# The second half of w_in by seven products instead of eight, with its scale measured during attention

## The chip, the cores and the metric

One core of one Trainium2 chip runs the whole kernel. The metric is the device time of the launch in microseconds, the median over the runs shown, lower being better. Five engines work from queues of their own and meet only at semaphores: TensorE (matrix products; PE in the profile, and PEld for the loading of its stationary operand), VectorE (DVE), ScalarE (ACT), GpSimd (POOL) and SyncE (SP, which issues most DMAs). Each takes its instructions in the order in which they were written; one that waits holds up all behind it on that engine.

## The reference, cut to what matters

The input x has 2048 tokens of 1024 features. Two blocks follow each other, each on a normalized input and added back to it:

```
h  = x + A(layernorm(x))     # causal attention in 4 segments of 512 tokens, 32 heads, with a running memory
h2 = h + B(layernorm(h))
B(x):  z  = gelu(x @ w_in)              # w_in: 1024 x 3584
       z1 = z[:, :1792]                 # first half
       z2 = layernorm(z[:, 1792:])      # second half, normalized per token
       g  = w_sp @ z2 + b_sp            # w_sp: 2048 x 2048, mixes tokens
       out = (z1 * g) @ w_out           # w_out: 1792 x 1024
```

The change concerns the second half of x @ w_in, the 2048 x 1024 by 1024 x 1792 product in front of z2.

## The kernel before, in words

A recorder (`_Recorder`) keeps the operations of each engine in the order of the Python calls and works out the waits from the tiles that are read and written; the profile therefore gives line 210 for nearly everything, and one has to go by tile names. The order written in Python is the order on each engine; nothing is reordered later.

**Attention** is a loop of 32 steps, n = 0 to 31: segment s = n // 8, a group of four heads c = n % 8. A step issues three rounds of logits into PSUM banks 0 to 3 (`logits`; the third round also puts the memory product `om` there, `mem`), and ACT takes each round out with an exp into tile `e`; POOL then masks `e` (`affine_select`). DVE takes `om` out in `mem_norm` (tiles `rdm`, `tm`), and the logits of the next step overwrite these banks. The products of the step before (`pv`, banks 4 and 5) are taken out by DVE in `norm` (tiles `rd`, `ta`, `otok`). Between these stand fillers: the projections of the next step (`qk`, taken out by ACT, in segment 0 by DVE), and in slots f3 and f4 the V projection (taken out by ACT) or, in steps c = 2 to 5, the output projection of the segment before (`wo`, taken out by DVE into `hch`, followed by a layernorm in tasks that `bg_pop` advances). Fillers use banks 6 and 7 in turn. `phi_max` prepares the next step's `pqk` on DVE at the end of the step.

**z2 stage.** w_in's second half is loaded in four chunks of 448 columns (`win`). `z2_group(k, tc)` multiplies 128 tokens with one chunk in eight matmuls of 448 columns; ACT takes the bank out with a gelu into `Z2`, and `z2_stats` sums it on DVE for the layernorm (`bn_stats`, tile `zst`). 4 chunks x 16 token tiles x 8 give 512 matmuls, 48 of them as fillers of steps 30 and 31. Between them stands `wo` of the last segment. Beside them run: the squares of w_sp's 16 row blocks on ACT (`sp_norm`, tile `sj`), the maxima of w_in's first half on DVE (`wz_norm`, 14 reductions into `sqz`), its scaled f16 copies (`wz_half`), the differences of the normalized input (`hn_sum`, tiles `ht` and `z1x`) and sums of the weights on POOL (`sz_sum`).

**z1 stage.** The first half is already computed by seven block products instead of eight (a scheme of Strassen's kind): `z1_step(g, k)` is product k of group g, four matmuls of 512 columns; 14 groups of 7. Product 1 is copied by ACT to `zt`, and DVE adds it to the banks (five additions a group). The rest of the layernorm is applied to Z2 here, alternately on DVE and ACT (`z2_apply`).

Then follow the token mix (`gate`) for the first 1024 tokens, 16 output units, `gate` for the other 1024, and the last output products; all of these are as before in the change, up to the addresses of buffers.

Of the kernel before, what the change touches and what calls it, by code (L numbers as in the profile page):

```python
# [12 lines left out]
T = 2048  # L13
D = 1024
# [244 lines left out]
def bass_sequential_preLN__memory_aug_infini_attn__mixer_gmlp__prompt_kernel(  # L259
# [31 lines left out]
    class Bump:  # L291
# [4 lines left out]
        def __call__(self, name, shape, dt):  # L296
# [50 lines left out]
    ZSTG = [tens("zstg%d" % i, [128, 448], F32, (134 + 2 * i) * K) for i in range(4)]  # L347
    XCH = [b2("xch%d" % i, [128, D], BF16) for i in range(4)]
# [4 lines left out]
    E = [[b2("e%d%d" % (k, i), [128, 4, w], BF16) for i, w in enumerate((512, 512, 256))] for k in range(2)]  # L353
    TA = b2("ta", [128, 4, 4, 32], F32)
    TM = [b2("tm%d" % i, [128, 4, 4, 32], F32) for i in range(2)]
    V = b2("v", [128, 4, H, 34], BF16)
    OTOK = [b2("otok%d" % i, [128, 4, D], BF16) for i in range(2)]


    WIN = [tens("win%d" % i, [128, 8, 512], BF16, o * K) for i, o in enumerate((46, 54, 190, 198))]  # L360
# [9 lines left out]
          for k, o in ROLES + (("t1", 118), ("t2", 190), ("t3", 22), ("t4", 38))}  # L370
    SS = tens("ss", [128, 4, 8, 128], F16, 30 * K)
    Z1X = tens("z1x", [128, 14, T], F16, 62 * K)
    HT = [{1: Z1X[:, 1:5, 1024:1536], 2: Z1X[:, 1:5, 1536:2048], 3: Z1X[:, 8:12, 1024:1536],
           4: Z1X[:, 8:12, 1536:2048]},
          {1: tens("ht1", [128, 4, L], F16, 190 * K), 2: tens("ht2", [128, 4, L], F16, 194 * K),
           3: tens("ht3", [128, 4, L], F16, 38 * K), 4: tens("ht4", [128, 4, L], F16, 198 * K)}]
    SZ = [tens("sz%d" % i, [128, 4, 128], F16, o * K) for i, o in enumerate((58, 59, 60, 61, 204))]
    ZT = [tens("zt%d" % i, [128, L], F32, o * K) for i, o in enumerate((4, 6, 8, 10, 202, 12))]
# [7 lines left out]
    SQ = b3("sq", [128, 16], F32)  # L386
    SQZ = b3("sqz", [128, 14], F32)
# [8 lines left out]
    TMP = {k: tens("tmp_" + k, [128, L], F32, (4 + 2 * i) * K)  # L396
           for i, k in enumerate(("s1", "s1b1", "s1b2", "u2", "u3"))}
    VB = tens("vb", [128, L], BF16, 61 * K)
    SJ = [tens("sj%d" % i, [128, T], BF16, (4 + 4 * i) * K) for i in range(2)]
    BROW = [tens("brow%d" % i, [128, L], BF16, (205 + i) * K) for i in range(2)]  # L400
    WO0 = [tens("w_out0%d" % i, [128, 7, 512], BF16, o * K) for i, o in enumerate((54, 198))]
    WO1 = [tens("w_out1%d" % i, [128, 7, 512], BF16, o * K) for i, o in enumerate((30, 4))]
# [3 lines left out]
    SY = [tens("sy%d" % i, [128, 4, 7, 128], F16, o * K) for i, o in enumerate((190, 126))]  # L406
    FIN = [tens("fin%d" % i, [128, 512], BF16, o * K) for i, o in enumerate((37, 11, 12, 13))]
# [13 lines left out]
    def next_bank():  # L421
        b = rot["banks"][rot["n"] % len(rot["banks"])]
        rot["n"] += 1
        return b
# [382 lines left out]
    CH = [(FH + 448 * k, 448) for k in range(4)]  # L807

    def win_load(k):
        lo, w = CH[k]  # L810
        sp.dma_start(WIN[k][:, :, 0:w], wcols(B_w_in, lo, lo + w))

    zs, zq, staged = [], [], []

    def z2_group(k, tc, stage=None):
        s, tcl = divmod(tc, 4)
        b = next_bank()
        wi = WIN[k]
        mm8(PS[:, b, 0:448], lambda i: HNT[s][:, i, tcl * 128:(tcl + 1) * 128], lambda i: wi[:, i, 0:448])
        if stage is None:  # L820
            z2_gelu(k, tc, PS[:, b, 0:448])
        else:
            act.activation(ZSTG[stage][:], PS[:, b, 0:448], ACTF.Copy)
            staged.append((k, tc, ZSTG[stage][:]))

    def z2_gelu(k, tc, src):
        act.activation(Z2[:, tc, k * 448:(k + 1) * 448], src, ACTF.Gelu_apprx_tanh)
        zs.append((k, tc))

    def z2_stats():  # L830
        k, tc = zs.pop(0)
        dve.bn_stats(ZST[:, tc, k, :], Z2[:, tc, k * 448:(k + 1) * 448])
        if k == 3:
# [13 lines left out]

    LAST = NSEG * NQ - 1
    for n in range(LAST + 1):
# [13 lines left out]
        elif c < 2:  # L863
            f3, f4 = [("v", s, 2 * c, 1)], [("v", s, 2 * c + 1, 1)]
        elif c < 6:
            f3, f4 = [("wo", s - 1, c - 2, 0)], [("wo", s - 1, c - 2, 1)]
        elif c == 6:
            f3, f4 = [("z2", 0, 4, 0)], [("z2", 0, 5, 1)]
        else:
            f1, f2 = [("z2", 0, 6, 2)], [("z2", 0, 7, 3)]  # L870
            f3, f4 = [("z2", 0, 0)], [("z2", 0, 1)]
# [14 lines left out]
        if n == 0:  # L886
# [3 lines left out]
            f3 = [("vmm", 0, 0, 1, 6, 2, 8), ("vout", 0, 0, 1, 6)]  # L890
        logits(n, 0)
# [12 lines left out]
        if n < LAST:  # L904
            phi_exp(n + 1)
        if n == 0:
# [9 lines left out]
        bg_pop()  # L916
        if n == 0:
# [3 lines left out]
        if n in (24, 26):  # L921
            win_load((n - 24) // 2)
    pv(LAST)
    xr_load(4 * (NSEG - 1))


    rot["banks"] = [0, 1, 2, 3, 6, 7, 4, 5]
    rot["n"] = 0
    win_load(2)

    pool.memset(ONES[:], 1.0)
    pool.memset(MHZ[:], -0.5)

    def sp_norm_load(r):
        sp.dma_start(SJ[r % 2][:], B_w_sp[r * 128:(r + 1) * 128, :])

    def sp_norm(r):
        act.activation(SJ[r % 2][:], SJ[r % 2][:], ACTF.Square, accum_out=SQ[:, r:r + 1])

    def scale_of(k, n, b):  # L940
        b = next_bank() if b is None else b
        pe.matmul(PS[:, b, 0:n], ONES[:], SQB[:, 0:n], start=True, stop=True)
        dve.tensor_reduce(out=TOT[:], in_=PS[:, b, 0:n], axis=mybir.AxisListType.X, op=ALU.add)
        dve.tensor_single_scalar(TOT[:], TOT[:], 1e-30, ALU.max)
        if k:
            dve.reciprocal(TOP[:], TOT[:])
        else:
            pool.tensor_tensor(TOP[:], TOT[:], MHZ[:], ALU.pow)

    def scale_end(k):  # L950
        dve.tensor_single_scalar(TOP[:].bitcast(I32), TOP[:].bitcast(I32), 0x7F800000, ALU.bitwise_and)
        dve.tensor_single_scalar(SC[k][:], TOP[:], 8192.0, ALU.mult)
        dve.reciprocal(INV[k][:], SC[k][:])

    def wz_load(q):
        w = 256 if q < 3 else 128
        for i in range(2):
            lo = 896 * i + 256 * q
            sp.dma_start(WZ[q][:, :, i, :], wcols(B_w_in, lo, lo + w))

    def wz_norm(q, r):
        v = WZ[q][:, 2 * r:2 * r + 2, :, :] if q < 3 else WZ[q][:, 4 * r:4 * r + 4, :, :]
        dve.tensor_reduce(out=SQZ[:, 4 * q + r:4 * q + r + 1], in_=v.rearrange("p c i w -> p (c i w)"), axis=mybir.AxisListType.X, op=ALU.max,
                          apply_absolute_value=True)

    def wz_half(q, h):
        dve.tensor_single_scalar(WZH[q][:, 4 * h:4 * h + 4], WZ[q][:, 4 * h:4 * h + 4], SC[1][:], ALU.mult)

    def hb(j, k, p):
        return HNT[2 * p + k][:, 4 * j:4 * j + 4, :]  # L970

    def hn_sum(p, t, h, eng=dve):
        a, b = {1: (hb(0, 1, p), hb(0, 0, p)), 2: (hb(1, 1, p), HT[p][1][:]),
                3: (hb(1, 1, p), hb(0, 1, p)), 4: (hb(1, 0, p), HT[p][2][:])}[t]
        s = slice(2 * h, 2 * h + 2)
        eng.tensor_tensor(HT[p][t][:, s, :], a[:, s, :], b[:, s, :], ALU.subtract)

    def wz_blk(i, j, fc):
        o = 128 * (fc % 2)
        return WZH[fc // 2][:, 4 * j:4 * j + 4, i, o:o + 128]  # L980

    def sz(g, k):
        return SZ[k - 1 + (k == 4 and g % 2)][:]

    def sz_sum(g, k):
        fc = g % 7
        a, b, op = {1: (wz_blk(1, 0, fc), wz_blk(1, 1, fc), ALU.add), 2: (sz(g, 1), wz_blk(0, 0, fc), ALU.subtract),
                    3: (wz_blk(0, 0, fc), wz_blk(1, 0, fc), ALU.subtract),
                    4: (wz_blk(0, 1, fc), sz(g, 2), ALU.subtract)}[k]
        pool.tensor_tensor(sz(g, k), a, b, op)  # L990

    aux = {}

    def at(q, f, *a):
        aux.setdefault(q, []).append((f, a))

    for r in range(16):
        q = (37 * r + 15) // 16
        at(q, sp_norm, r)
        if r < 14:  # L1000
            at(q, sp_norm_load, r + 2)
    at(37, pool.tensor_copy, SQB[:, 0:16], SQ[:])
    for k in range(12):
        at(k + 1, wz_norm, (1, 2, 0)[k // 4], k % 4)
    for k in range(8):
        at(3 + 2 * k, hn_sum, 0, (1, 2, 3, 4)[k // 2], k % 2)
    at(18, wz_norm, 3, 0)
    at(19, wz_norm, 3, 1)
    at(20, pool.tensor_copy, SQB[:, 0:14], SQZ[:])
    at(25, scale_of, 1, 14, None)  # L1010
    at(25, scale_end, 1)
    for k in range(8):
        at(26 + k, wz_half, k // 2, k % 2)
    for k in range(4):
        at(28 + 2 * k, hn_sum, 1, 1 + k // 2, k % 2)
    for k in (1, 2, 3, 4):
        at(28 + k, sz_sum, 0, k)

    todo = [(0, 2), (0, 3), (0, 8), (0, 9), 0, (0, 10), 1, (0, 11), 2, (1, 0), 3]
    todo += [(1, tc) for tc in range(1, 4)] + [(0, tc) for tc in range(12, NTC)]  # L1020
    todo += [(1, tc) for tc in range(4, NTC)] + [(k, tc) for k in (2, 3) for tc in range(NTC)]
    for it in todo:
        if isinstance(it, int):
            for half in range(2):
                wo(NSEG - 1, it, half)
                bg_pop()
            continue
        z2_group(*it)
# [505 lines left out]
```

## Time and profile before

| | before |
|---|---|
| median of 3 runs | 754.44 us (754.37 to 754.87) |
| the profiled execution | 753.9 us, its span 752.2 us |
| TensorE busy | 747.5 us, 99% of the span |
| DVE, ACT, POOL busy | 559.3, 421.3, 297.0 us |
| attention, 18.2 to 302.8 us | TensorE busy throughout |
| z2 stage, 302.8 to 404.4 us | 536 matmuls; DVE 82.9, ACT 59.4, POOL 19.3 us busy |
| z1 stage, 404.4 to 489.2 us | 394 matmuls; DVE 69.0, ACT 67.7, POOL 70.0 us busy |

The span is what the profiler saw between the first and the last instruction; the execution's own time is 1.7 us longer. An engine's busy time is the union of its instructions. A busy TensorE is not one at its peak: matmuls overlap, and the duration shown of one (352 or 379 ns) is not the time that it takes from the next; that is read from the start of a row of many to the start of the row after.

### The profile page before, as it was taken

How to read it: one execution, taken by the hardware profiler on the slowest of the kernel's cores; microseconds unless marked ns; L12 is line 12 of the kernel's file. 1: busy time of each engine (PE TensorE's matmuls, PEld its weight loads, DVE VectorE, ACT ScalarE, POOL GpSimd, SP SyncE). 2: the span in 40 equal slices, each digit the busy share in tenths (PEclk: the TensorE clock that was granted, in tenths of full speed). 3: DMA queues.
4: the chain of work that ended last, by engine and by line, in shares of the span. 5: the costliest groups of instructions: out<-in, count | busy, mean ns of one | idle time of the engine just before them, and what ended most of it. 6: DMA issues, size and time to landing. Idle time of an engine off the chain costs nothing.

```text
span 752.2 us, 13510 instructions
## 1 busy us (share of the span) xinstructions
PE 747.5 (99%) x5470; PEld 358.8 (48%) x5470; DVE 559.3 (74%) x1013; ACT 421.3 (56%) x519; POOL 297.0 (39%) x450
## 2 busy tenths in 40 slices
PE   8999999999999999999999999999999999999998
PEld 4445455555555445545554444444444444444444
DVE  5585589768975576667988796997885465989776
ACT  6777877787777767324994879733231445300000
POOL 2564456555654334010049888622220001222342
PEclk9999999999999999999999999999999999999999
DMA  9654556444523331669650027320019950001211
GB/s 303 177 159 88 85 82 135 99 74 91 120 58 81 118 84 44 162 178 262 196 169 0 1 45 138 56 98 1 0 23 155 269 185 28 0 1 43 78 50 57
DMA packets 136783, 75.09 MB, mean 100 GB/s; under 512 B 98064, under 2 KB 126480, under 8 KB 136720
## 3 DMA queue, kind: packets, MB, share of 16 engines
q1 hardware_dynamic: 129184, 67.14, 36.9%
q10 hardware_dynamic: 7536, 7.08, 3.3%
q8 instruction: 43, 0.70, 0.4%
q14 instruction: 20, 0.16, 0.1%
HBM read 42.74 MB, written 8.39 MB: 68 GB/s over the span
## 4 chain that ended last, share of the span: by engine, by line
PE 98%; DMA 1%; ACT 0%; DVE 0%; ACTq 0%; DVEq 0%; issue 0%
PE ps L210 98%; DMA wv<-in_A_wv_dram 1%; ACT L210 0%; DVE fin L210 0%; ACTq L210 0%; DVEq L220 0%; ACT rdm L210 0%
## 5 line engine op out<-in xcount | busy, mean ns | idle before, releaser
L210 ACT ACTIVATE e<-ps 128x2048 bf16<-128x2048 f32 (+1 forms) x96 | 152.6, 1590 | 41.7 <-PE ps L210 41.5
L210 POOL TENSOR_SCALAR_AFFINE_SELECT e<-e 128x512 bf16<-128x512 bf16 x128 | 90.6, 720 | 131.6 <-ACT e L210 131.5
L210 PE MATMUL ps<-win,hnT 128*128 128x448 bf16 x512 | 98.4, 352 | 0.0
L210 POOL TENSOR_TENSOR tmp_s1b<-tmp_s,brow 128x512 f32<-128x512 f32 x28 | 36.9, 1322 | 121.3 <-DVE tmp_u L210 62.5
L210 PEld LDWEIGHTS ps<-win,hnT 128*128 128x128 bf16 x512 | 49.6, 98 | 46.3 <-issue 0.2
L210 PE MATMUL ps<-xnT,wk 128*128 128x512 bf16 x256 | 60.8, 380 | 0.0
L210 PE MATMUL ps<-xnT,wq 128*128 128x512 bf16 x256 | 60.5, 379 | 0.0
L210 PE MATMUL ps<-wv,xnT 128*128 128x512 bf16 x256 | 59.7, 380 | 0.3 <-DVE xnT L210 0.3
L210 DVE TENSOR_TENSOR zt<-ps,zt 128x512 f32<-128x512 f32 x70 | 48.2, 690 | 15.6 <-PE ps L210 12.3
L210 PE MATMUL ps<-wo,oT 128*128 128x512 bf16 x256 | 58.0, 379 | 0.0
L210 ACT ACTIVATE z<-ps 128x448 bf16<-128x448 f32 x60 | 30.4, 545 | 33.4 <-PE ps L210 33.4
L210 PE MATMUL ps<-w_out,z1T 128*128 128x512 bf16 x224 | 48.6, 379 | 0.0
L210 PEld LDWEIGHTS ps<-v,e 128*128 128x128 bf16 x1280 | 38.8, 96 | 14.0 <-issue 6.5
L210 DVE BATCH_NORM_STATS2 zst<-z 128x6 f32<-128x448 bf16 x64 | 37.7, 607 | 7.8 <-ACT z L210 7.8
L210 DVE RECIPROCAL rd<-ps 128x16 f32<-128x16 f32 x32 | 8.0, 250 | 47.1 <-PE ps L210 46.9
L210 PE MATMUL ps<-v,e 128*128 128x33 bf16 x1280 | 42.2, 178 | 0.0
L210 ACT ACTIVATE tmp_s<-ps,invy 128x512 f32<-128x512 f32 x7 | 4.8, 688 | 64.9 <-POOL tmp_s1b L210 36.1
L210 POOL TENSOR_TENSOR sz<-wzh 128x512 f16<-128x512 f16 x28 | 34.4, 1230 | 16.9 <-DVE wzh L210 8.5
L210 PEld LDWEIGHTS ps<-wo,oT 128*128 128x128 bf16 x256 | 24.0, 98 | 27.6
L210 PEld LDWEIGHTS ps<-xnT,wk 128*128 128x128 bf16 x256 | 22.6, 98 | 29.9 <-issue 5.0
L210 ACT ACTIVATE z1T<-zt,inv 128x512 bf16<-128x512 f32 x42 | 29.0, 716 | 13.1 <-DVE zt L210 13.1
L210 PEld LDWEIGHTS ps<-wv,xnT 128*128 128x128 bf16 x256 | 23.1, 98 | 27.2 <-DVE xnT L210 0.7
(204 smaller groups left out, 1462.3 us busy)
## 6 DMA issues: line engine op xcount, KB each, us to landing
sj<-in_B_w_sp_dram SPq DMA_DIRECT2D x16, 512.0 KB, 3.5
xch<-in_A_x_dram SPq DMA_DIRECT2D x16, 256.0 KB, 3.5
xr<-in_A_x_dram SPq DMA_DIRECT2D x16, 256.0 KB, 4.0
out_dram<-hch SPq DMA_DIRECT2D x16, 256.0 KB, 2.5
win<-in_B_w_in_dram SPq DMA_DIRECT2D x4, 896.0 KB, 5.4
wz<-in_B_w_in_dram SPq DMA_DIRECT2D x6, 512.0 KB, 8.3
wo<-in_A_wo_dram SPq DMA_DIRECT2D x1, 2048.0 KB, 8.5
fin<-out_dram ACTq DMA_DIRECT2D x16, 128.0 KB, 3.0
```

What stands on the lines that cost most here:

```text
L210: ins = getattr(e, op.name)(*op.args, **op.kw)
```

## The change

1. **Seven products in z2.** Tokens are taken in two halves p of 1024, columns in two pairs of chunks c and c + 2, features in two halves. A group (p, c, t) is four token tiles' worth of one such product by blocks: seven products of four matmuls, 448 columns wide, instead of four times eight matmuls. Two of the sixteen groups, (0, 0, 0) and (0, 0, 1), are left as plain `z2_group`s; they are the fillers of steps 30 and 31 and the first two of the stage. The weights are scaled to f16 first (`w_half`), block sums made on DVE (`w_sum`, `w_perm`), and the input differences `hn_sum` of both halves are made earlier, the first half's at the end of attention.
2. **Seeds in PSUM, in both halves of w_in.** ACT copies product 1 from its bank into the bank of products 6, 7 and 4, which then add to it; the additions of product 1 on DVE go. A bank that no full-width product has written yet gets one extra matmul first (`wide`, `full`). Banks are now handed out from a list of free ones in place of a fixed turn.
3. **Products far apart.** `OFF2` sets how many places lie between a product and those that need its result; it replaces `offs` in z1. The gelus of results that pass through DVE are issued one place later (`late`).
4. **Norms in attention.** The maxima and squares that set the scales of w_in (now of all of it, 16 pieces) and of w_sp (14 of 16 rows) are taken at the ends of attention steps from step 6 on (`pieces`): 18 reductions on DVE, 12 squares on ACT, each with a load of 448 or 512 KB on SP's queue into buffers `NB`. The remaining two rows are four half-rows on ACT in z2.
5. **No long GpSimd operations in z2**, apart from four `sz_sum`s near its end; the layernorm's applications are all on DVE now.
6. Many buffers move to other addresses.

In the list of places of the z2 stage (98 of them, `seq2`), `jobs2` hangs the other work on places: the two first plain groups and two `w_half` at 0 to 3, four weight sums from 7 to 17, the `wo` tiles at 8, 10, 12 and 14, eight `hn_sum` at 22 to 36, three more weight sums at 32, 46 and 50, `z2_apply` from 54 on, `wz_half` at 58, 62, 92 and 94, the loads of w_in's first half at 26 and 75. `z2_stats` runs by a credit: 0.3 a place up to 40, then 0.62.

```
 def next_bank(hold=False):
+        if free:
+            b = free.pop(0)
+            if not hold:
+                free.append(b)
+            return b
...
+    pieces = {}
+    for i, (n, k, q) in enumerate(((6, 0, dve), (6, 1, dve), (7, 0, dve), (7, 1, dve), (8, 0, dve), (14, 1, dve),
+                                   (15, 0, dve), (15, 1, dve), (16, 0, dve), (17, 1, dve), (10, 0, act), (11, 1, act),
+                                   (12, 0, act), (13, 1, act), (18, 2, act), (19, 3, act))):
+        pieces.setdefault(n, []).append((NB[k], SQZ, i, q))
+    for i, (n, k, q) in enumerate(((22, 2, dve), (23, 3, dve), (23, 4, dve), (24, 2, dve), (24, 5, dve), (25, 4, dve),
+                                   (25, 6, dve), (26, 6, dve), (20, 2, act), (21, 3, act), (26, 5, act), (27, 4, act),
+                                   (28, 5, act), (29, 4, act))):
+        pieces.setdefault(n, []).append((NB[k], SQ, i, q))
...
     for n in range(LAST + 1):
+        piece_loads(n + 1, act)
         logits(n, 0)
...
             phi_exp(n + 1)
+        piece_norms(n, act)
...
         fill(f4)
         bg_pop()
+        if n == 25:
+            scale_of(16)
+        piece_norms(n, dve)
+        piece_loads(n + 1, dve)
...
+        if n == 26:
+            scale_end(1)
+            w_half(0)
+        if n == 28:
+            w_half(2)
+        if n == 29:
+            w_sum(0, 3, WS[0, 0])
+            w_sum(0, 2, WS[0, 0])
+        if n == 30:
+            w_sum(0, 4, WS[0, 0])
+            hn_sum(0, 1, 0)
+            hn_sum(0, 1, 1)
...
+        if n == LAST:
+            hn_sum(0, 2, 0)
+            hn_sum(0, 2, 1)
+            hn_sum(0, 3, 0)
+            hn_sum(0, 3, 1)
+            w_sum(0, 1)
+            hn_sum(0, 4, 0)
+            hn_sum(0, 4, 1)
...
+    G2 = [(0, 0, 2), (0, 0, 3)] + [(p, c, t) for p, c in ((0, 1), (1, 0), (1, 1)) for t in range(4)]
+    OFF2 = {1: -6, 6: 0, 5: 1, 2: 2, 7: 4, 4: 10, 3: 12}
...
+    def z2_step(q, k):
+        p, c, t = G2[q]
...
+        if k in (1, 5):
+            zb2[q, r] = next_bank(True)
+        if k == 1:
+            zb2[q, 1] = next_bank(True)
+        for i in range(4):
+            pe.matmul(v[r], kb[:, i, t * 128:(t + 1) * 128], ka[:, i, :], start=(k in (1, 5) and i == 0),
+                      stop=(i == 3), skip_group_check=True)
+        wide.add(zb2[q, r])
+        if k in (2, 3, 4):
+            free.append(zb2[q, r])
+        todo, late[:] = late[:], []
+        if k == 1:
+            if zb2[q, 1] not in wide:
+                pe.matmul(v[1], kb[:, 0, 0:128], ka[:, 0, :], start=False, stop=False, skip_group_check=True)
+                wide.add(zb2[q, 1])
+            act.activation(v[1], v[0], ACTF.Copy)
+        elif k == 6:
+            act.activation(u2, v[1], ACTF.Copy)
+        elif k == 5:
+            act.activation(u3, v[2], ACTF.Copy)
+        elif k == 7:
+            dve.tensor_tensor(u3, v[1], u3, ALU.add)
+            late.append(lambda: z2_gelu(c + 2, 8 * p + 4 + t, u3))
+        elif k == 2:
+            z2_gelu(c, 8 * p + t, v[0])
+        elif k == 4:
+            z2_gelu(c + 2, 8 * p + t, v[1])
         else:
+            dve.tensor_tensor(u2, v[2], u2, ALU.add)
+            late.append(lambda: z2_gelu(c, 8 * p + 4 + t, u2))
...
+    seq2 = sorted((7 * q + OFF2[k], q, k) for q in range(len(G2)) for k in OFF2)
+    credit = 0.0
+    for n, (x, q, k) in enumerate(seq2):
+        if n == len(seq2) - 2:
+            z1_step(0, 1)
+        z2_step(q, k)
+        for f, a in jobs2.pop(n, ()):
+            f(*a)
+        credit = min(credit + (0.3 if n < 40 else 0.62), 2)
+        if credit >= 1 and len(zs) > 1:
+            z2_stats()
+            credit -= 1
...
     def z1_step(g, k):
...
         if k == 1:
-            act.activation(s1, b, ACTF.Copy)
-        if k == 6:
-            dve.tensor_tensor(u2, b, s1, ALU.add)
+            act.activation(bank(zb[g, 1]), b, ACTF.Copy)
+        elif k == 6:
+            dve.tensor_copy(u2, b)
+        elif k == 5:
+            act.activation(u3, b, ACTF.Copy)
...
-    for g in range(8):
-        on(g, 6, lambda: zq and z2_apply())
-        on(g, 4, lambda: zq and z2_apply(True))
+    for g in range(11):
+        on(g, 7, lambda: zq and z2_apply())
```

## The prediction

> **What bounds the kernel now.** I read the busy times and the chain first, then the stages by windows, then rows of single instructions. From the page:
>
> ```profile
> PE 747.5 (99%) x5470; PEld 358.8 (48%) x5470; DVE 559.3 (74%) x1013; ACT 421.3 (56%) x519; POOL 297.0 (39%) x450
> PEclk9999999999999999999999999999999999999999
> PE ps L210 98%; DMA wv<-in_A_wv_dram 1%; ACT L210 0%; DVE fin L210 0%; ACTq L210 0%; DVEq L220 0%; ACT rdm L210 0%
> ```
>
> TensorE is the whole chain, at full clock. Whether it is at its peak the windows by stage tell (PE, PEld, DVE, ACT, POOL busy and their counts), with the timeline of TensorE:
>
> ```profile
> 302.78:404.39 101.61, 101.61 (x536) 51.67 (x532) 82.93 (x145) 59.35 (x93) 19.30 (x39) 1.00 0.63 179
> 404.39:489.20 84.81, 84.81 (x394) 38.13 (x393) 69.00 (x101) 67.69 (x88) 70.03 (x69) 1.00 0.30 53
> ...
> 308.83 3.62 PE L210 MATMUL ps<-wo,oT 128*128 128x512 bf16 x16
> 312.29 1.68 PE L210 MATMUL ps<-win,hnT 128*128 128x448 bf16 x8
> ...
> 327.19 50.10 PE L210 MATMUL ps<-win,hnT 128*128 128x448 bf16 x264
> 377.12 0.17 PE L210 MATMUL ps<-sqb,ones 128*128 128x14 bf16 x1
> ```
>
> From start to start, 264 matmuls of 448 columns took 49.93 us, 0.189 each, and 16 of 512 columns 3.46 us, 0.216 each. With these, z2 is 464 x 0.189 + 64 x 0.216 = 101.5 us, z1 392 x 0.216 = 84.8 us: the windows, without a gap. So a matmul less is worth its 0.189 us as long as nobody makes TensorE wait, and DVE has 18.7 us to spare in z2.
>
> What the other engines' work costs is in the rows by shape (busy, mean ns):
>
> ```profile
> L210 DVE TENSOR_TENSOR zt<-ps,zt 128x512 f32<-128x512 f32 x70 | 48.2, 690 | 15.6 <-PE ps L210 12.3 <-ACT z1T L210 1.9
> L210 DVE BATCH_NORM_STATS2 zst<-z 128x6 f32<-128x448 bf16 x64 | 37.7, 607 | 7.8 <-ACT z L210 7.8
> L210 DVE TENSOR_REDUCE sqz<-wz 128x1 f32<-128x1024 bf16 x14 | 16.8, 1202 | 3.5 <-DMA wz<-in_B_w_in_dram 3.5
> L210 DVE TENSOR_REDUCE hsum<-xch 128x1 f32<-128x512 bf16 x1 | 0.7, 686 | 2.1 <-DMA xch<-in_A_x_dram 2.1
> L210 ACT ACTIVATE sj<-sj 128x2048 bf16<-128x2048 bf16 x16 | 30.7, 1916 | 9.0 <-DMA sj<-in_B_w_sp_dram 9.0
> ```
>
> The room for norms in attention is in DVE's timeline; step 16, from its rd to the end of tm, and the logits of step 17 on TensorE:
>
> ```profile
> 157.91 0.26 DVE L210 RECIPROCAL rd<-ps 128x16 f32<-128x16 f32 x1 [3.09 <-PE ps L210]
> ...
> 162.24 0.69 DVE L210 TENSOR_TENSOR tm<-ps,rdm 128x512 f32<-128x512 f32 x1
> ...
> 163.40 0.40 PE L210 MATMUL ps<-qk 32*128 32x512 bf16 x4
> ```
>
> DVE idles 3.09 us before rd; then its list is full to the end of tm (162.93), and the logits that overwrite what tm read start 0.47 us later. What is put before rd and takes over 3.09 + 0.47 us makes TensorE wait.
>
> **TensorE's part.** z2 becomes 8 plain groups x 8 + 14 x 28 = 456 matmuls for 512: 56 x 0.189 = 10.6 us less. Added: one 448-column matmul for a bank not yet written full width (0.19) and in z1 some 64-column ones and the 494-column one of the scale (0.3). Net **-10.1**. Operands of f16 with bf16 go at z1's 0.216 already.
>
> [...]
>
> **Norms in attention, DVE.** By 1202 ns for 1024 elements and 686 for 512, a reduction takes 1.97 us over 1792 and 2.23 over 2048. They stand last in a step, so they run early in the next, in front of its rd. A single one (9, 15, 17, 18, 23) fits the 2.3 to 3.1 us idle there. Two:
> - step 7: 3.9 us into 3.0; 0.96 and 1.43 us idle follow: nothing.
> - step 8: from 80.2 to 84.2, rd due at 82.51; 0.30 idle to tm, which ended 1.04 before the logits: 1.7 - 0.3 - 1.0 = 0.4.
> - step 16: 154.82 + 3.95 = 158.8, rd due at 157.91: 0.9 late, 0.47 gap: 0.5 with the hand-over.
> - steps 24 to 26: 4.5 to 4.9 us (with the small scale operations) into 3.4 to 3.9, then 0.88 to 1.36 idle before rdm: nothing, but full to the brim.
> - step 26 also: the scale's matmul takes a bank of the two in turn, so the K projection gets the bank that slot f4 has just filled and waits for ACT's 0.6 us: 0.45.
> - step 27: one reduction 2.23, three small ones 0.46, w_half 1.15 (4096 elements take 1.28): from 259.78 to 263.6, rd due at 260.87; less 1.36 idle, 1.4 late. There hch ended at 265.93 and the K projection into its bank began at 266.69: 1.4 - 0.76 = 0.7.
> - steps 29 to 31: w_half 1.15, two w_sum of 1.09 (1024 elements take 0.68, 4096 2.29), then 2.45 us: all under the idle.
> - after step 31: 5.2 us in front of the last norm, which leaves bank 4 at 307.5; TensorE wants it at 308.3.
>
> Sum **+2.0**; bounds 0 (every hand-over half a microsecond easier) and 6 (steps 24 to 26 each 1 late and w_sum slowed beside GpSimd as otok is, 1.08 for 0.69).
>
> **ACT, SP and POOL in attention.** A square with its accumulator read takes 1.9 to 2.1 us; ACT idles 1.76 us before a step's first exp (2.19 in segment 3), and that exp ended 0.42 before TensorE wanted its banks: nothing; uncovered, 0.3 x 12. The 30 loads (3.5 us to landing for 512 KB) wait on SP for the reduction that frees their buffer; behind them stand pk's transposes, wanted a step later, and in step 26 the xr load, held to 252.7 and wanted at 265.25: nothing; uncovered, its 4.0 us once. POOL's copy of the sums waits for DVE until 243.9 in step 25, its masks behind it 2.8 us; pv wants them at 250.06: nothing.
>
> **z2's other engines.** ACT: three copies of 0.55, gelus 2 x 0.55 and 2 x 0.6, 4.0 us a group for TensorE's 28 x 0.189 = 5.3: room; the seed, at least five places of 0.756 before its use, is not waited for. DVE, from 301.2 on: differences and last norm 7.1, w_half 2.3, seven weight sums 7.6, hch 8 x 0.68, layernorm of wo 8.7, hn_sum 8 x 0.68, additions 28 x 0.62 = 17.4, bn_stats 48 x 0.61 = 29.3, aggregates 2.1, applications 8 x 0.77, wz_half 3.7: 95.2 us. TensorE's stage is 408 x 0.189 + 13.8 + 0.2 = 91.2, ending 92.8 after 301.2. DVE is over by 2.4, most of it in places 58 to 97: 33.9 us of work in 30.2. An addition after product 7 may be 3.5 us late before product 4, six places on, waits. With 1 us of backlog from the first part: 1 + 3.7 - 3.5, taken as **+1.0**; bounds 0 (in a row, instructions of 0.69 follow each other at 0.61) and 5 (5% more work on DVE).
>
> **The seam and z1.** DVE's copy after z1's first product 6 must be done before product 7, three places of 0.87 on; entering 3.5 late, it costs 0.9; ACT's first seed has 1.5 us for its 0.6: 0.1. **+1.0**, bounds 0 and 2. In z1 DVE has 20 us less to add. ACT has 4.0 us a group for 6.06, but in groups 8 and 9 eight scalings of 1.14 on top: 18.7 us in 14.7, and product 6 waits from 4.3 late on: **+0.2**, bounds 0 and 1.5.
>
> **The sum.** -10.1 + 2.0 + 1.0 + 1.0 + 0.2 = -5.9. The profiled execution took 753.9 us (span 752.2 and 1.7 around it), so 748.0; the median of before is 0.5 above that execution, so **748.5**.
>
> The granted clock is 1.00 in every window, through PE's 8 tenths in the first slice too, so I price a stall at its length. [...]
>
> **Rivals.**
> - *All hidden*, 754.4 - 10.1 = **744.3**. For it: every stall above is a difference of under 1.1 us between nearly equal times. Against: step 27.
> - *DVE bounds z2*: the 5 us bound there, 2.0 and 1.2 elsewhere: 754.4 - 10.1 + 8.2 = **752.5**. For it: 95.2 us of work in 92.8. Against: the fast rows in a stretch without POOL (hn_sum 0.68 there, 1.64 beside POOL).
> - *Slower*: the reductions stretch beside POOL's masks, as otok does (1.08 for 0.69, 1.56 times). Then two of them take 2.2 to 2.5 us more; steps 8 and 16 lose 2.2 each, 24 to 26 1.5 each, 27 1.25: 10.1 us on top of the forecast, **758.6**. It decides from about 1.45 times on, where the stalls pass 11.6. Against: bn_stats, one input too, took 0.68 to 0.70 in all of attention.
>
> **How the numbers follow.** Forecast 0.45 (its own range 746 to 751.5), all hidden 0.22, DVE bounds z2 0.17 (751.5 to 754.5), reductions stretch 0.12, others 0.04. Of these, faster by over 0.2% (a time under 752.9; 0.2% is about what a measurement of this kernel can tell from no change) is 0.45 + 0.22 + 0.10 = 0.77; within 0.2%, 0.08; slower, 0.15. The range goes from all hidden, with the spread of runs below it, to the end of DVE bounds z2: 743.9 to 754.5.
>
> **What would show it.** Right: 457 matmuls of 448 columns; 0.189 from start to start in z2; steps 8, 16, 26 and 27 (from their logits to the next) longer by 0.4 to 0.7 and the others as before; TensorE waiting for DVE in the last third of z2. Wrong: reductions over 2.4 us, logits waiting in most steps with two pieces, TensorE waiting for ACT's seeds or for w_half behind a late load.

## The result and the profile after

The changed kernel takes 747.67 us (747.33 to 747.86, four runs), the kernel before, on the same chip, 754.40 (753.53 to 754.87). The ratio is 0.9912, with a 95% interval of 0.9894 to 0.9929; the forecast was 748.5. The profiled execution took 747.58 us, its span 745.9, so the span lost 6.3 us against that of before.

Where the 6.3 us lie is read by cutting both spans at three instructions of TensorE: the first logits, the first matmul of z2 after the last `pv`, and the first of `gate`.

| us | before | after | difference |
|---|---|---|---|
| start to first logits | 18.22 | 18.79 | +0.57 |
| attention | 284.56 | 286.18 | +1.62 |
| z2 and z1 | 186.48 | 177.94 | -8.54 |
| gate to the end | 262.91 | 262.94 | +0.03 |

The first row lies inside a spread that no edit accounts for: in the ten more profiles behind the experiments below that stretch took 18.4 to 20.8 us. As there is a single profile of the kernel before, at 18.2, it isn't shown that none of the 0.57 us comes from the change. Busy times, granted clock and chain by lines after:

```profile
PE 738.8 (99%) x5419; PEld 353.9 (47%) x5419; DVE 595.8 (80%) x1041; ACT 439.4 (59%) x567; POOL 296.1 (40%) x443
PEclk9999999999999999999999999999999999999999
PE ps L210 93%; DVE sqz L210 1%; DMA wv<-in_A_wv_dram 1%; DVE stats L210 1%; ACT e L210 0%; DVE hch L210 0%; POOL sz L210 0%; DVE tm L210 0%; DVE otok L210 0%; DVE sq L210 0%; DVE rdm L210 0%; DVE pqk L210 0%; DVE rd L210 0%; DVE etmp L210 0%; ACT qk L210 0%
```

The chain, 98% TensorE before, is broken in a few places now. Followed in order of time (start, length, what), it names each place at which TensorE waited and for whom:

```profile
80.79 1.94 DVE sqz L210
82.75 2.02 DVE sqz L210
...
88.39 0.70 DVE tm L210
...
155.87 2.02 DVE sqz L210
157.92 2.02 DVE sqz L210
...
249.42 0.59 ACT v L210
...
264.11 1.05 DVE wih L210
...
268.14 0.69 DVE hch L210
268.87 48.02 PE ps L210 x513
316.91 0.70 DVE hch L210
317.66 82.39 PE ps L210 x425
400.13 1.46 POOL sz L210
401.65 1.16 POOL sz L210
402.95 339.79 PE ps L210 x1584
```

Those are steps 8, 16, 26 and 27 of attention, place 8 of the z2 list, and the seam. The time of a piece isn't a loss (4 us of reductions at 80.79 stood mostly in idle time); what was lost is in the lengths of the steps, from their logits to the next:

| step | before | after | predicted loss | measured |
|---|---|---|---|---|
| 8 | 9.49 | 10.06 | 0.4 | 0.58 |
| 16 | 9.42 | 9.59 | 0.5 | 0.17 |
| 26 | 9.19 | 9.61 | 0.45 | 0.42 |
| 27 and 28 (hch's wait falls just behind the first logits of 28) | 18.38 | 18.81 | 0.7 | 0.44 |

All other steps are what they were, to 0.01 us. Two windows, z2 and z1 (us; busy time and instructions of PE, PEld, DVE, ACT, POOL; granted clock; DMA):

```profile
304.96:398.15 93.19, 92.41 (x485) 46.54 (x482) 82.08 (x145) 59.78 (x111) 15.54 (x29) 1.00 0.38 97
398.15:482.91 84.76, 84.47 (x394) 37.88 (x392) 61.42 (x95) 64.11 (x97) 71.09 (x69) 1.00 0.30 53
```

In z2 DVE is at work 82.1 of 93.2 us, and TensorE stands still for only some 1.1 us, nearly all of it at one place, shown here in TensorE's timeline around it:

```profile
314.99 1.89 PE L210 MATMUL ps<-wo,oT 128*128 128x512 bf16 x8
317.66 1.90 PE L210 MATMUL ps<-wo,oT 128*128 128x512 bf16 x8 [0.78 <-DVE hch L210]
```

and in DVE's:

```profile
315.10 1.09 DVE L210 TENSOR_TENSOR wse<-z1x,wsf 128x1792 f16<-128x1792 f16 x1
316.91 0.69 DVE L210 TENSOR_TENSOR hch<-xr,ps 128x512 bf16<-128x512 bf16 x1 [0.72 <-PE ps L210]
```

DVE wasn't late: it idled 0.72 us until the first eight matmuls of the `wo` tile had ended, and began at once. TensorE's next eight needed that bank, the only one free, and started 2.67 us after the first eight instead of 1.72: 0.95 us. At the seam it was GpSimd that came late, as its timeline shows:

```profile
400.13 1.45 POOL L210 TENSOR_TENSOR sz<-wzh 128x512 f16<-128x512 f16 x1 [6.86 <-PE ps L210]
401.65 1.15 POOL L210 TENSOR_TENSOR sz<-sz,wzh 128x512 f16<-128x512 f16 x1
```

It had idled 6.86 us before the two `sz_sum`s that `z1_step` issues behind product 5 (they overwrite what products 6 and 5 of the first group read); TensorE's product 6 of the second group waited 0.46 us for the second. What DVE's maxima cost is in the rows by shape (number, then busy us and mean ns):

```profile
L210 DVE TENSOR_REDUCE sqz<-nb 128x1 f32<-128x1792 bf16 x10 | 20.1, 2013 | 0.1
L210 DVE TENSOR_REDUCE sq<-nb 128x1 f32<-128x2048 bf16 x8 | 18.2, 2274 | 0.1
```

The reductions took 2.01 and 2.27 us, where 1.97 and 2.23 had been worked out from shorter ones: they don't stretch beside GpSimd's masks. The pair at 230.91, with a mask of 0.63 us beside it, took 4.60 us, and so did the pair at 240.32, with nothing on GpSimd beside it.

### The profile page after: what moved, and what is told of

Its sections match the earlier page's. It is cut to its first block, busy times and chain, and to the rows that moved or that the text cites. A ratio compares the mean times of both kernels' runs of the same rounds, so it can differ in the third digit from the quotient of the medians.

```text
span 745.9 us, 13501 instructions
## 1 busy us (share of the span) xinstructions
PE 738.8 (99%) x5419; PEld 353.9 (47%) x5419; DVE 595.8 (80%) x1041; ACT 439.4 (59%) x567; POOL 296.1 (40%) x443
## 4 chain that ended last, share of the span: by engine, by line
PE 93%; DVE 4%; ACT 1%; DMA 1%; issue 0%; POOL 0%; DVEq 0%
PE ps L210 93%; DVE sqz L210 1%; DMA wv<-in_A_wv_dram 1%; DVE stats L210 1%; ACT e L210 0%; DVE hch L210 0%; POOL sz L210 0%; DVE tm L210 0%; DVE otok L210 0%; DVE sq L210 0%; DVE rdm L210 0%; DVE pqk L210 0%; DVE rd L210 0%; DVE etmp L210 0%; ACT qk L210 0%
## 5 line engine op out<-in xcount | busy, mean ns | idle before, releaser
L210 DVE TENSOR_TENSOR zt<-ps,zt 128x512 f32<-128x512 f32 x28 | 19.1, 686 | 22.2 <-PE ps L210 19.3
L210 ACT ACTIVATE qk<-ps 128x512 bf16<-128x512 f32 x48 | 28.7, 599 | 12.9 <-PE ps L210 12.9
L210 PE MATMUL ps<-qk 32*128 32x128 bf16 (+3 forms) x512 | 34.5, 302 | 0.7 <-DVE tm L210 0.5
L210 ACT ACTIVATE tmp_s<-ps,inv 128x512 f32<-128x512 f32 x7 | 4.8, 687 | 50.9 <-POOL tmp_s1b L210 37.9
L210 PEld LDWEIGHTS ps<-xnT,wq 128*128 128x128 bf16 x256 | 23.5, 98 | 22.9 <-issue 0.2
L210 PEld LDWEIGHTS ps<-w_out,z1T 128*128 128x128 bf16 x224 | 21.7, 98 | 26.2
```

What stands on the lines that cost most here:

```text
L210: ins = getattr(e, op.name)(*op.args, **op.kw)
```

## The experiments

Ten runs of nine more kernels, each an edit of the changed one. Times are medians, ratios go against the kernel before on the same chip, with 95% intervals.

### 1. Attention without the maxima

The 18 maxima of `piece_norm` on DVE are left out, and constants stand in for them; the loads and ACT's squares stay.

```
-        else:
-            dve.tensor_reduce(out=o[:, i:i + 1], in_=v, axis=mybir.AxisListType.X, op=ALU.max,
-                              apply_absolute_value=True)
...
+            pool.memset(SQZ[:, 0:10], 0.17)
+            pool.memset(SQ[:, 0:8], 0.0017)
```

> This kernel is the changed one without the 18 reductions that VectorE makes in attention; their columns hold constants instead, so the scales are not those of the data. The 30 loads, the 12 squares on ScalarE and all else stay. Theory (the reductions stand in front of VectorE's hand-overs and make TensorE wait): step 8 goes back from 10.06 to 9.49 us, step 16 from 9.59 to 9.42, steps 27 and 28 from 9.36 and 9.45 to 9.19; step 26 keeps its 9.61, since that one is the scale's matmul taking a bank in turn. Attention 286.2 to 285.0, the median 747.7 to 746.5. Rival (the loads, on SyncE's queue and in the DMA engines, are what delays the steps): all steps stay as they are, 747.7.

Measured: 746.47 us (746.36 to 747.29), ratio 0.9893 (0.9876 to 0.9909). Steps 8, 16, 27 and 28 are back at 9.48, 9.42, 9.19 and 9.19; step 26 stays at 9.61. Attention takes 284.99 us, 1.19 less than after the change; z2 and z1 together 177.96, as before the edit. DVE's timeline in step 8 without the maxima:

```profile
83.03 0.26 DVE L210 RECIPROCAL rd<-ps 128x16 f32<-128x16 f32 x1 [2.27 <-PE ps L210]
...
86.79 0.69 DVE L210 TENSOR_TENSOR tm<-ps,rdm 128x512 f32<-128x512 f32 x1
```

and with them, in the changed kernel:

```profile
80.71 4.06 DVE L210 TENSOR_REDUCE sqz<-nb 128x1 f32<-128x1792 bf16 x2
84.69 0.25 DVE L210 RECIPROCAL rd<-ps 128x16 f32<-128x16 f32 x1
...
88.39 0.69 DVE L210 TENSOR_TENSOR tm<-ps,rdm 128x512 f32<-128x512 f32 x1
```

Two maxima of 4.06 us in 2.27 us of idle time make `rd` 1.66 late and `tm` 1.60; the step became 0.58 longer, so 1.02 of it was slack at the logits. That the loss of step 26 stays shows that it is of another kind.

### 2. Products close together, seeds kept

```
-    OFF2 = {1: -6, 6: 0, 5: 1, 2: 2, 7: 4, 4: 10, 3: 12}
+    OFF2 = {1: -5, 6: 0, 5: 1, 7: 3, 2: 4, 4: 6, 3: 12}
```

> The spacing of products of the kernel before (places -5, 0, 1, 3, 4, 6, 12 for products 1, 6, 5, 7, 2, 4, 3), in z2 and z1, with the seeds kept. Theory (VectorE runs some microseconds behind TensorE in z2, and the distance of six places from product 7 to product 4 is what hides it; three places leave 2.3 us less the addition's 0.6): z2 and z1 together 177.9 to 181 or 184, the median 751 to 754. Rival (the changed kernel's trace shows only 1.8 us of waits in these stages, so VectorE is mostly on time and three places are enough): at most 1 us longer, 747.7 to 748.7.

Measured: 752.06 us (751.24 to 752.61), ratio 0.9963 (0.9948 to 0.9977). z2 and z1 by windows:

```profile
304.80:398.77 93.97, 93.14 (x482) 45.90 (x481) 82.48 (x145) 59.77 (x112) 16.37 (x29) 1.00 0.38 95
398.77:486.57 87.80, 84.80 (x387) 37.50 (x393) 62.82 (x95) 62.92 (x96) 71.25 (x69) 1.00 0.30 51
```

The same work on every engine, and 3.8 us more: 0.8 in z2, 3.0 in z1, as waits for DVE's `zt`, the longest 1.27 us. With three places from product 6 to product 7 and three from there to product 4, DVE's list decides when TensorE goes on; with four and six, as in the change, hardly ever.

### 3. Seven products in z2 without seeds

Product 1 is copied to a tile and added by DVE, five additions a group, at the old spacing, as z1 was before; two `hn_sum`s stand some places later.

```
         if k == 1:
-            act.activation(v[1], v[0], ACTF.Copy)
+            act.activation(s1, v[0], ACTF.Copy)
         elif k == 6:
-            act.activation(u2, v[1], ACTF.Copy)
-        elif k == 5:
-            act.activation(u3, v[2], ACTF.Copy)
+            dve.tensor_tensor(u2, v[1], s1, ALU.add)
         elif k == 7:
-            dve.tensor_tensor(u3, v[1], u3, ALU.add)
+            dve.tensor_tensor(u3, v[1], s1, ALU.add)
+            dve.tensor_tensor(u3, v[2], u3, ALU.add)
...
         elif k == 4:
-            z2_gelu(c + 2, 8 * p + t, v[1])
+            dve.tensor_tensor(s1, v[1], s1, ALU.add)
```

> Seven products in z2, but made as z1 was before: product 1 is copied to SBUF and VectorE adds it to the three banks (five additions a group for two), with the old spacing; z1 as in the changed kernel. Three additions of 0.61 us in 14 groups are 25.7 us more on VectorE, which was busy for 82 of 93 us. Theory (VectorE's load decides whether the saved matmuls show): z2 becomes VectorE's, 12 to 15 us longer, the median 760 to 763, slower than before the change. Rival (only the count of matmuls matters, the additions find room in z1, which lies behind): at most 2 us longer, 750.

Measured: 763.31 us (762.87 to 764.85), ratio 1.0116 (1.0101 to 1.0131): slower than the kernel before, although TensorE has its 56 matmuls less. The window of z2:

```profile
306.94:414.62 107.68, 94.68 (x481) 45.07 (x480) 103.78 (x186) 49.32 (x83) 15.04 (x29) 1.00 0.33 84
```

and TensorE's waits in it (us in total, times, longest):

```profile
PE ps L210 <- DVE zp L210: 12.7, 15, 2.2
```

DVE is full, 103.8 of 107.7 us. Of the 14.5 us that z2 is longer, experiment 2 gives 0.8 to the spacing alone; the rest needs the additions. So in z2 the seeds are what pays: without them, at the old spacing, the seven products lose. The additions at the wide spacing were not run.

### 4. The old scheme in z1 alone, and where its loss sits

```
-            act.activation(bank(zb[g, 1]), b, ACTF.Copy)
+            act.activation(s1, b, ACTF.Copy)
...
-            dve.tensor_copy(u2, b)
+            dve.tensor_tensor(u2, b, s1, ALU.add)
...
-    for x, g, k in sorted((7 * g + OFF2[k], g, k) for g in range(14) for k in OFF2):
+    OFFS = {1: -5, 6: 0, 5: 1, 7: 3, 2: 4, 4: 6, 3: 12}
+    for x, g, k in sorted((7 * g + OFFS[k], g, k) for g in range(14) for k in OFFS):
```

> The seeds and the wide spacing undone in z1 alone: five additions a group on VectorE for two and a copy, products placed as before; z2 as in the changed kernel. VectorE gets some 1.4 us more in each of 14 groups, 61.4 to 81 us busy of 84.8. Theory (in z1 VectorE had room before the change, so the seeds are worth nothing there): z1 at most 1 us longer, 747.2 to 748.7; a gain of up to 0.5 is possible since the wait for GpSimd's sum at the start of z1 (0.46) comes from the wide spacing. Rival (seeds matter in both stages): 3 us or more longer, 751.

Measured: 752.88 us (752.09 to 753.65, nine runs), ratio 0.9975 (0.9965 to 0.9984). z1 took 89.68 us for 84.76; the theory, at most 1 us, fell. Yet DVE isn't full in that window:

```profile
397.75:487.43 89.68, 85.89 (x392) 37.07 (x390) 74.86 (x124) 56.45 (x82) 71.23 (x69) 1.00 0.32 51
```

DVE's timeline in one group shows why it is late all the same:

```profile
424.84 0.61 DVE L210 BATCH_NORM_STATS2 zst<-z 128x6 f32<-128x448 bf16 x1
425.49 0.26 DVE L210 BATCH_NORM_AGGREGATE zmv<-zst 128x2 f32<-128x24 f32 x1
425.67 0.63 DVE L210 TENSOR_TENSOR zt<-ps,zt 128x512 f32<-128x512 f32 x1
```

The addition of 425.67, after product 6, ends at 426.30; TensorE's product 7, which overwrites what it read, starts at 426.35 and could have at 426.05. In front of it stand the statistics that z1 inherits from z2. The kernel before had the same scheme in z1 in 84.8 us, with no statistics there and half of the applications on ACT.

A run meant to move the statistics kept their order by a slip in the edit, and so repeats this kernel:

> The run with the old scheme in z1, with one more edit: the layernorm statistics that z1 inherits from z2 are issued after products 6 and 2 of a group instead of after 4 and 3, so that they no longer stand on VectorE's list in front of the addition that product 7 waits for. Theory (the order on VectorE's list cost the 4.9 us, not the number of additions: VectorE was busy 74.9 of 89.7 us there): the waits of 0.3 us at product 7 in nearly every group go, z1 comes back from 89.7 to 85 to 86.5 us, the median to 748 to 749.5 us, within 2 us of the changed kernel. Rival (the five additions a group and the applications, all on VectorE, are themselves too much at the old spacing, wherever the statistics stand): z1 stays at 88.5 us or more, the median at 751.5 us or more.

Its 752.82 us (752.21 to 755.0, ten runs), ratio 0.9976 (0.9965 to 0.9987), says how well such a number stands, and nothing on the question. Then with the edit:

```
-        for k in (4, 3):
+        for k in (6, 2):
             on(g, k, lambda: zs and z2_stats())
```

> The run with the old scheme in z1 with the edit that its repetition lacked: the statistics that z1 inherits are issued after products 6 and 2 of a group instead of after 4 and 3. VectorE's list is then the addition after 3, the one after 4, the one after 6, and only then the statistics. Theory (the statistics in front of the addition after product 6 make the wait at product 7): the waits of 0.3 us at product 7 in the groups from the fourth on go (six of them, 1.8 us), those of 1.27, 0.79 and 0.54 us at the same product lose at least 0.5 us each, and the 0.72 us near the end, behind additions for w_sp, stays: z1 goes from 89.7 us to 86 to 87, the median to 749.3 to 750.3 us. Rival (five additions a group at the old spacing are too much for VectorE wherever the statistics stand): the waits move to another product, z1 stays at 88.7 us or more, the median at 752 us or more.

Measured: 753.90 us (753.52 to 755.96, ten runs), ratio 0.9993 (0.9983 to 1.0002): 1 us slower still, z2 and z1 184.00 for 182.84. The waits at product 7 went to 0.1 to 0.2 us, as expected, but a new one came, on TensorE four times like this:

```profile
424.37 1.90 PE L210 MATMUL ps<-z1x,sz 128*128 128x512 f16 x8 [0.78 <-POOL sz L210]
```

with the cause in GpSimd's timeline:

```profile
420.82 0.22 POOL L210 TENSOR_SCALAR zrs<-zmv 128x1 f32<-128x1 f32 x1 [1.11 <-DVE zmv L210]
421.13 0.57 POOL L210 TENSOR_TENSOR zrs<-zrs,mhz 128x1 f32<-128x1 f32 x1
421.66 1.16 POOL L210 TENSOR_TENSOR sz<-wzh 128x512 f16<-128x512 f16 x1
422.89 1.42 POOL L210 TENSOR_TENSOR sz<-sz,wzh 128x512 f16<-128x512 f16 x1
```

`z2_stats` also issues two small GpSimd operations that wait for DVE's aggregate. With the aggregate later, GpSimd stood 1.11 us before a 0.22 us operation, and the weight sums of the next product 6 behind it came 0.94 us late. So one more run left the first statistic of z1 out of its hook, which puts the aggregates after product 2:

```
-            on(g, k, lambda: zs and z2_stats())
+            if (g, k) != (0, 6):
+                on(g, k, lambda: zs and z2_stats())
```

> The run before (old scheme in z1, statistics after products 6 and 2) with the first statistic of z1 left to the next hook, so that the one that completes a token tile, with its aggregate and GpSimd's two operations for the standard deviation behind it, falls after product 2 and no longer after product 6. Theory (what was saved at product 7 came back because GpSimd, whose list is in order, waited 0.5 to 1.1 us for an aggregate that VectorE reached later, and its weight sums behind it were late for product 6 by 0.94 us four times): these four waits go, the others stay, z2 and z1 together go from 184.0 to 180 to 181 us, the median from 753.9 to 749.8 to 751 us. Rival (GpSimd has no room in z1 wherever its wait stands, or VectorE hasn't): the sums or the additions wait elsewhere, z2 and z1 together stay above 182.5 us and the median above 752.3 us.

Measured: 751.43 us (751.1 to 752.08), ratio 0.9961 (0.9947 to 0.9975); z2 and z1 181.74. Between the two expectations: the four waits for GpSimd became one of 0.75 us, and in every second group product 7 waits 0.54 to 0.90 us for DVE again, where the aggregate now stands ahead of the additions. The order of the lists is worth 2.3 us over the three arrangements (182.84, 184.00 and 181.74), but none came near the 177.9 us of the changed kernel. With seeds at the same spacing (experiment 2) z1 took 87.80 us, in the window of the same kind here 88.56: by this subtraction most of the 3.8 us that remain go with the old spacing, and the two more additions a group make 0.8 in the best order tried, 1.9 in the first. It is a subtraction and not an experiment of its own, since experiment 2 had the old spacing in z2 as well. Both explanations are right in part; an order in which the old scheme loses nothing wasn't found, and the old scheme with half of the applications on ACT and no statistics left over, as it ran in 84.8 us before, was not tried on top of the new z2.

### 5. GpSimd kept busy in z2

```
+        if n % 2 and n < 76:
+            pool.tensor_tensor(SCR[:], HNT[0][:, n % 8, :], HNT[1][:, n % 8, :], ALU.subtract)
```

> The changed kernel with 38 additional GpSimd subtractions of 128x512 in z2, one at every second place up to place 75, whose result nothing reads (some 1.2 us each). Theory (GpSimd beside VectorE stretches VectorE's operations with two inputs in SBUF and its fast copies: 0.68 to 1.15 and 1.64 us for hn_sum in the kernel before): some 25 such operations in z2 (hn_sum, weight sums, applications, scalings) take 0.4 to 1 us more each, 10 to 20 us on VectorE, which has 11 to spare; z2 2 to 7 us longer, the median 750 to 755. Rival (VectorE's list in z2 has room enough, or GpSimd is the one that waits): at most 0.5 us longer.

Measured: 757.96 us (757.31 to 759.43), ratio 1.0044 (1.0029 to 1.0059), slower than the kernel before and more than was expected. z2 by its window:

```profile
305.39:408.56 103.17, 95.33 (x483) 46.31 (x481) 96.41 (x145) 59.48 (x111) 66.63 (x67) 0.98 0.34 87
```

DVE does the same 145 instructions in 96.4 us instead of 82.1. Rows by shape, first with GpSimd busy, then in the changed kernel:

```profile
L210 DVE TENSOR_TENSOR ht<-hnT 128x1024 f16<-128x1024 bf16 x2 | 3.3, 1634 | 0.0
L210 DVE TENSOR_TENSOR z1x<-hnT,z1x 128x1024 f16<-128x1024 bf16 x4 | 4.5, 1160 | 0.0
L210 DVE TENSOR_TENSOR zp<-ps,zp 128x448 f32<-128x448 f32 x28 | 16.6, 607 | 1.5 <-PE ps L210 1.5
```

```profile
L210 DVE TENSOR_TENSOR ht<-hnT 128x1024 f16<-128x1024 bf16 x2 | 1.4, 682 | 0.0
L210 DVE TENSOR_TENSOR z1x<-hnT,z1x 128x1024 f16<-128x1024 bf16 x4 | 2.6, 682 | 0.0
```

With these operations the window is 10 us longer, and the gain is gone. That shows what a GpSimd busy for 66.6 us does to z2; the kernel before had it busy for 19.3 us there, and what those operations alone would cost beside the new z2 was not run, so how much part 5 of the change is worth stays open. Up to 1.7 us of the 10 were the clock (an estimate, half of the 3.41 us in the last section). Outside z2 this one execution is another 1.4 us longer behind z1, with a wait of 1.26 us for a load of `w_out` whose cause stays open.

### 6. The `wo` tile one place later

```
-        at(8 + 2 * i, wo_tile, i)
+        at((9, 10, 12, 14)[i], wo_tile, i)
```

> The first tile of the last output projection stands at place 9 of z2 for place 8. Theory (at place 8 three groups hold seven of the eight PSUM banks, so both halves of the tile get the one bank left, and the second waits for VectorE to empty it, 0.95 us; at place 9 one more bank is free): the wait goes, z2 0.9 us shorter, 746.8. Rival (VectorE's own backlog at the end of attention delays the emptying): the wait moves along, the time stays within 0.2 us of 747.7.

Measured: 746.79 us (746.0 to 747.18), ratio 0.9890 (0.9873 to 0.9907). The wait for `hch` is gone, z2 and z1 take 176.99 us, 0.95 less. That is what the shortage of banks at place 8 predicts: one place later a second one has come free. DVE's list, which would have been the other suspect, has the same operations in the same order.

### 7. Five mends together

The `wo` tile as above; in the first group of z1 product 5 ahead of 6, each sum issued after the product that reads its buffer; one of step 7's maxima in step 9; `w_half(0)` a step later; and the turn of the two filler banks set back after the scale's matmul of step 25.

```
+            rot["n"] -= 1
...
+        if n == 27:
             w_half(0)
...
+    for x, g, k in sorted((7 * g + OFF2[k] - 1.5 * ((g, k) == (0, 5)), g, k) for g in range(14) for k in OFF2):
```

> The changed kernel with five mends: the first tile of the output projection at place 9 (0.95 us); product 5 of the first z1 group ahead of product 6, so that GpSimd's sums for the second group start a product earlier (0.46); one of step 7's two reductions at the end of step 9 (0.58); the first scaling of w_in after step 27 for step 26 (0.44); and the bank turn set back by one after the scale's matmul, so that the K projection gets the bank of that matmul (0.2 to 0.4 of 0.42). Theory (the waits seen in the trace are on the path, each with its own cause): 2.5 us less, 745.2. Rival (waits taken away come back at the next narrow place): 0.5 to 1 us less, 747.

Measured: 745.27 us (745.13 to 745.38), ratio 0.9871 (0.9851 to 0.9890), ahead of both kernels. Steps 8, 27 and 28 have the lengths of before, step 26 is 0.03 above, step 16 keeps its 0.17; attention takes 284.77 us, z2 and z1 176.54, with some 0.4 us of waits left. Of the five only the turn set back touches step 26, so the 0.42 us there were the bank that its filler got.

## Why the prediction was right, step by step

- **TensorE's part, -10.1: right.** The trace has 457 matmuls of 448 columns, 456 and the one for a bank not yet written. z2 and z1 lost 8.54 us and hold 1.8 us of waits where before held 0.2: 10.2 without them. The seeds of z2, copies of product 1, took that one extra matmul of 448 columns, and those of z1 three of 64 columns; no run had seeds without these.
- **Attention, +2.0: 1.6,** in the four places named and nowhere else. In steps 24 and 25, "full to the brim", nothing was lost. Step 16 was over-priced (0.5 for 0.17), step 8 under (0.4 for 0.58), step 27 over (0.7 for 0.44). In step 16 `rd` came 0.80 us late, but `tm` only 0.58: `otok` between them took 0.87 us where it had taken 1.08. The mechanism, what exceeds the idle time before `rd` less the slack at the logits, is shown by experiment 1; step 26's, the turn of two banks, by experiment 7.
- **z2's other engines, +1.0: 1.1, for another reason.** The forecast had DVE over-full, 95.2 us of work, late in the last third. DVE was busy 82.1 us and hardly late, and the sign that the prediction had named, TensorE waiting for DVE in the last third, did not come; 0.95 of the 1.1 us came from place 8, where one bank was free. The term that failed is the sum of DVE's work: it adds full durations, but in a row each instruction starts before the one ahead has ended, as DVE's timeline of the changed kernel shows late in z2, 0.61 long and 0.52 to 0.53 apart:

```profile
385.83 0.61 DVE L210 TENSOR_TENSOR zp<-ps,zp 128x448 f32<-128x448 f32 x1
386.35 0.62 DVE L210 BATCH_NORM_STATS2 zst<-z 128x6 f32<-128x448 bf16 x1
386.88 0.61 DVE L210 TENSOR_TENSOR zp<-ps,zp 128x448 f32<-128x448 f32 x1
387.41 1.28 DVE L210 TENSOR_SCALAR z2h<-z,zmv,zrs 128x1792 f16<-128x1792 bf16 x1
```

The durations themselves were forecast well. Those of the instructions that start in z2's window add up to 90.8 us, and with the overlaps counted once to 82.0: 8.8 us of the 13 by which 95.2 exceeds the busy time. Most of the rest is no error of price: the list also holds work in front of z2's first matmul and just behind its end (from 303.4 to 400 us the durations add up to 94.2). The prediction has the overlap (0.69 at 0.61) and uses it only for the lower bound. The bank shortage was no term at all: the prediction counts engines' time, and not how many banks are held at each place.
- **The seam, +1.0: 0.46, for another reason.** DVE's copy wasn't late, since its list wasn't; GpSimd's sums, queued behind product 5, were. **z1, +0.2: about 0.25, for other reasons.** ACT's scalings, the forecast's reason, show no wait. By the times of the trace 0.11 us stand behind a sum of GpSimd's, which ended at 463.61 with the product behind it starting at 463.75, and 0.16 in the last group, where only one product is left to stand between 7 and 4 and DVE's addition ended at 481.11, 0.06 before product 4.
- **The rivals.** *All hidden*, 744.3, is 1.0 us below experiment 7, whose start was 0.8 longer than that of before and where attention has 0.2 left. *DVE bounds z2* was far off, with 11 us to spare, but experiments 3 and 5 show that edge: 41 more instructions or a busy GpSimd and DVE does bound it, both times slower than before. *Slower* is refuted: the reductions took 2.01 and 2.27 us.

By stages the forecast was 1.0 us high, nearly all of it attention's 0.4 and the seam's 0.5. The medians show 0.8, by two offsets that nearly cancel: the start of the profiled execution was 0.57 longer, which no term had, and the median after lies 0.1 above that execution where 0.5 had been added. z2's term had its size by chance.

## What to carry to other kernels

When TensorE is the bound and a cheaper product scheme is at hand, its worth can hang on what the scheme puts on the engine that empties PSUM: here the same 56 matmuls fewer gave 6.7 us with seeds and wide spacing, and lost 8.6 with additions and the old spacing in z2. Price a list by start-to-start times, not by durations (0.53 for 0.61 us late in z2), and beside the engines' time count the PSUM banks held at each place of the order (0.95 us at place 8). A statistic moved to free one queue can hold up another one through a small operation that waits for it (0.94 us in experiment 4): follow each to all queues on which it issues something.

## What the runs showed of the hardware

**A clock halved for 3.41 us.** In experiment 5, three windows of 3.41 us in a row (PE first, then PEld, DVE, ACT, POOL; granted clock third from the end):

```profile
381.30:384.72 3.42, 3.39 (x18) 1.51 (x16) 3.35 (x7) 1.18 (x3) 1.98 (x4) 1.00 0.78 210
384.72:388.13 3.41, 1.25 (x6) 0.52 (x7) 3.38 (x7) 2.51 (x5) 3.25 (x5) 1.00 0.00 0
388.13:391.54 3.41, 3.41 (x11) 1.37 (x9) 3.38 (x7) 2.76 (x6) 3.33 (x5) 0.50 0.00 0
```

After a window in which TensorE was busy 1.25 of 3.41 us, because of two waits of 0.95 and 1.24 us, the clock was half for the whole next one, matmuls came 0.37 us apart (0.19 before the waits), and in the one behind that, 391.54 to 394.95, it was whole again (1.00). All four executions of this kernel have a mean granted clock of 0.998. The profiled execution of experiment 3 has such a stretch too, at its start, long before z2 (the first row is cut at 5.00):

```profile
5.00:8.48 3.48, 1.85 (x19) 1.02 (x17) 2.65 (x7) 2.52 (x5) 0.00 (x0) 1.00 1.05 366
8.48:11.89 3.41, 3.41 (x11) 1.31 (x10) 1.56 (x4) 2.16 (x4) 0.96 (x3) 0.50 1.18 296
```

There too 11 matmuls filled a halved row, and the clock was 1.00 again from 11.89 on; this execution's first logits came latest, at 20.8 us. On the other side, 309.62 to 313.04 in experiment 5 had one wait of 2.07 us and 1.42 us busy, and the clock stayed (1.00 there and in the row behind). So neither the longest wait nor the busy time of these rows decides by itself: a wait of 1.24 us in experiment 5 and 1.85 us busy in experiment 3 went before a halving, a wait of 2.07 us and 1.42 us busy did not, and what does decide isn't shown. The prediction prices stalls at their length: behind the two of experiment 5 the halved clock cost up to 1.7 us more, an estimate from half of the 3.41 us.

**What a busy GpSimd slows on DVE, and what not.** In z2 of experiment 5 additions with two operands in SBUF took from 0.67 us, as in the changed kernel, up to 1.64, a weight sum from 1.07 up to 2.05 (1.08 in the changed kernel), and an application 1.26 for 0.74 (medians). Additions with an operand in PSUM (0.61) and statistics (0.61) stayed. So did reductions beside GpSimd's masks in attention of the changed kernel (2.01 and 2.27; a pair 4.60 with a mask and without).
